# General path of a four-layer FNet and linear-attention kernel: input loads and output stores issued from ScalarE's queue instead of SyncE's

## The chip, the cores and the metric

The kernel runs on one NeuronCore of one Trainium2 chip. The metric is the device time of one execution in microseconds (us). Before the change three runs gave 745.84, 745.68 and 745.42 us, a median of 745.68 us.

## The reference

The input `x` is 2048 rows by 640 columns, float32. Four sublayers are applied in turn, each added to its own input: a Fourier layer, an attention layer, and both once more.

```python
x = x + _A_ref(_layernorm(x), dft_seq_re, dft_seq_im, dft_hid_re, dft_hid_im)
x = x + _B_ref(_layernorm(x), wqkv, wo)
# and the same two lines again

# _A_ref: y = Real(DFT_seq(DFT_hidden(x))), as dense products
a = einsum("bsd,ed->bse", x, dft_hid_re);  b = einsum("bsd,ed->bse", x, dft_hid_im)
y = einsum("ts,bse->bte", dft_seq_re, a) - einsum("ts,bse->bte", dft_seq_im, b)

# _B_ref: linear attention, 32 heads of 20, phi(t) = where(t > 0, t + 1, exp(t)) + 1e-6
kv = einsum("bhsd,bhse->bhde", phi(k), v);  z = einsum("bhsd->bhd", phi(k))
o = einsum("bhqd,bhde->bhqe", phi(q), kv) / (einsum("bhqd,bhd->bhq", phi(q), z) + 1e-6)
return o @ wo
```

The four Fourier matrices are inputs of the kernel, so the kernel may not assume what stands in them.

## The kernel before

The 2048 rows lie in 16 tiles of 128 rows (`X[0]` to `X[15]`), which stay on the chip through all four sublayers. The program has two ways to the result.

The fast path (`fast_path`, L1362 to L1453) uses the symmetries of a true Fourier matrix, which halve the products twice. While it computes, VectorE compares the whole Fourier matrices with their mirror images (class `Check`, L1324); `verdict` (L1331) reduces what it found to one integer, `ckflag`, during the last attention layer. The fast path loads `x` at L1372 and stores the result at L1424, both on SyncE's queue, which it has to itself: all 352 of the fast path's DMAs are issued there, in the order of the program. The order on the other engines is partly written out by hand, partly left to the planner, which simulates the schedule of a stretch of the program up to the next branch.

After the fast path, the flag is read by every engine into a register (L1502), and every engine branches on it (L1503):

```python
    bad = nc.values_load(flag, min_val=0, max_val=1)
    with tc.If(bad > 0):
        with ExitStack() as c2:
            general_path(k, c2, x, wqkv, wo, mask, (crt, cit, wrt, wit), out)
```

The general path (L1456 to L1484) does the whole computation again with plain dense products and overwrites the output. It is compiled into the program of every engine, between the branch and what follows it. An engine on which the flag is 0 jumps over it. Where it lands, a short stretch adds to the semaphores what the general path would have added: one instruction each on PE, DVE, ACT and POOL, and eight on SyncE, one for each of the eight semaphores that count DMA landings. Each of these eight first waits until all earlier DMAs counted by its semaphore have landed. Then come the closing instructions (marked L1626): on SyncE ten waits and three drains, on the others one or two of each, with two barriers over all engines.

Counted in the compiled program, the stretch that is jumped over holds 167 instructions on SyncE, 117 on DVE, 1015 on POOL, 1135 on ACT and 7310 on PE (each with its closing branch). SyncE's 167 are 95 DMA issues (16 loads of `x` at L1462, 20 of weights at L269, 12 at L526, 10 at L519, 20 small copies at L591, 17 stores at L1476), 71 instructions that only wait, and the branch. Three of the 71 stand ahead of the loads of `x` and one ahead of each store. ACT's 1135 contain 68 DMA issues already, for the Fourier matrices of the general path (L730, L754).

Of the kernel before, what the change touches and what calls it, by code (L numbers as in the profile page):

```python
# [17 lines left out]
HD = D // 2  # L18
# [1437 lines left out]
def general_path(k, ctx, x, wqkv, wo, mask, gen, out):  # L1456
    nc = k.nc
    xp = ctx.enter_context(k.tc.tile_pool(name="gxp", bufs=1))
    X = []
    for i in range(NT):  # L1460
        t = xp.tile([128, D], F32, name=f"gx{i}")
        nc.sync.dma_start(t, x[128 * i : 128 * i + 128, :])  # L1462
        X.append(t)
    order = list(range(NT))
    k.general, k.ve = True, Spared(k, ctx.enter_context(k.tc.tile_pool(name="near", bufs=3)))
    for layer in range(2):
        k.layer = 1
        layer_fourier_general(k, X, *gen)
        with ExitStack() as c2:
            for nm, b in (("tmp", 12), ("wp", 31), ("raw", 3), ("pqp", 16)):  # L1470
                setattr(k, nm, c2.enter_context(k.tc.tile_pool(name=k.nm(nm), bufs=b)))
            k.st = k.tmp

            def after(i, a, b):
                if layer == 1:
                    nc.sync.dma_start(out[128 * i : 128 * i + 128, HD * a : HD * b], X[i][:, HD * a : HD * b])  # L1476

            att = Attention(k, X, order, order, wqkv, wo, mask)
            for part in (1, 0):
                att.weights(part)  # L1480
            att.begin()
            att.begun()
            att.keys_values()
            att.outputs(after)  # L1484


@with_exitstack
def tile_kernel(
    ctx, tc, x, wqkv, wo, maskd, sign, ce, se, co, cex, wr, wi,
    ck0, ck1, ck2, ck3, ckr, cki, crt, cit, wrt, wit, out,  # L1490
):
    nc = tc.nc
    k = K(tc, ctx)
    mask = k.cst.tile([EC, EC], F32, name="mask")
    k.qd = ctx.enter_context(tc.tile_pool(name="qd", bufs=4))
    k.sm = ctx.enter_context(tc.tile_pool(name="sm", bufs=3))
    with ExitStack() as c2:
        c2.enter_context(tc.manual_schedule(engines={mybir.EngineType.SP}))
        flag = fast_path(
            k, c2, x, wqkv, wo, (mask, maskd), sign, (ce, se, co), cex, (wr, wi), (ck0, ck1, ck2, ck3), (ckr, cki), out  # L1500
# [5 lines that stand above are left out]
# [126 lines left out]
```

## Time and profile before

| what | value |
|---|---|
| median of three runs | 745.68 us (745.42 to 745.84) |
| the profiled execution's own time | 747.02 us |
| its span, first to last instruction | 745.0 us |
| outside the span | 2.0 us |
| busy share PE, DVE, ACT, POOL | 97%, 80%, 52%, 35% |
| granted TensorE clock, mean | 0.996 |
| instructions executed | 12,890 |
| DMA traffic of SyncE's queue | 104.20 MB |

An engine's name with a q (SPq, PEldq) means its sequencer, the part that waits, branches and issues DMAs. SP is SyncE. Rows of one line of code give the instruction, how often it ran, shortest, middle and longest duration in ns, and the start of the first and last in us. The rows of the profile with kind "instruction" are the DMA packets by which the engines fetch their own program.

### The profile page before, as it was taken

To read this page: it belongs to the slowest core of one execution; us is meant where nothing else is said; L and a number is where in the kernel's file an instruction comes from. 1 tells how busy PE (TensorE), PEld (TensorE's weight loads), DVE (VectorE), ACT (ScalarE), POOL (GpSimd) and SP (SyncE) were. 2 spreads that over 40 slices of the span, in tenths; PEclk is the share of its full clock that TensorE was granted. 3 is DMA by queue.
4 is the path that set the end of the run, shared out by engine and by line. 5 is a ranking of instruction groups with operands and counts; after the bars stand their busy time and mean duration, and the time that the engine had idled before them with its cause. 6 is when DMAs were issued, how large, how long until landed. Compare 5 with 4: busy or idle time off the path is not lost.

```text
span 745.0 us, 12890 instructions
## 1 busy us (share of the span) xinstructions
PE 723.1 (97%) x4762; PEld 691.4 (93%) x4762; DVE 599.6 (80%) x1147; ACT 384.4 (52%) x723; POOL 262.5 (35%) x293
## 2 busy tenths in 40 slices
PE   4999999999999999999999999999999999999997
PEld 1389999999999999899986999999999999999996
DVE  7998988868779786888987876967787887689973
ACT  7745654665445644455775347566532554453320
POOL 4237941331024311567772672136000010153310
PEclk9999999999999999999999999999999999999999
DMA  9332457562776826420001463654156653102653
GB/s 329 103 91 89 130 165 244 179 202 67 241 223 209 269 97 197 152 93 1 10 10 54 145 233 91 211 162 148 37 163 198 189 187 119 56 12 72 194 162 109
DMA packets 59006, 105.10 MB, mean 141 GB/s; under 512 B 5652, under 2 KB 23319, under 8 KB 58935
## 3 DMA queue, kind: packets, MB, share of 16 engines
q1 hardware_dynamic: 58935, 104.20, 43.8%
q8 instruction: 40, 0.66, 0.4%
q14 instruction: 31, 0.25, 0.1%
HBM read 78.99 MB, written 24.78 MB: 139 GB/s over the span
## 4 chain that ended last, share of the span: by engine, by line
PE 71%; DVE 15%; ACT 5%; DMA 3%; issue 2%; POOL 2%; SPq 1%; DVEq 0%; ACTq 0%; POOLq 0%
PE ps L250 48%; PE ps L355 16%; PE ps L1173 3%; PE ps L1099 2%; PE ps L201 1%; DVE w L189 1%; DVE t L189 1%; DMA raw<-in_wo 1%; DMA x<-in_x 1%; DVE t L622 1%; DVE ab L992 1%; DVE ps L615 1%; DVE x L644 1%; DMA raw<-in_wqkv 1%; PE ps L543 1%
## 5 line engine op out<-in xcount | busy, mean ns | idle before, releaser
L250 PE MATMUL ps<-w,t 128*128 128x320 f32 x2880 | 432.1, 310 | 0.6 <-DVE w L189 0.2
L250 PEld LDWEIGHTS ps<-w,t 128*128 128x128 f32 x2880 | 422.7, 188 | 1.9 <-DVE t L189 0.8
L355 PE MATMUL ps<-t,t 128*128 128x256 f32 (+1 forms) x640 | 139.8, 309 | 0.0
L1324 DVE CUSTOM_DVE_ANT_0 junk<-ck,ck 128x688 bf16<-128x688 f32 (+5 forms) x138 | 112.3, 813 | 7.4 <-DMA ck<-in_ck 6.2
L355 PEld LDWEIGHTS ps<-t,t 128*128 128x128 f32 x640 | 107.0, 188 | 0.0
L355 PE MATMUL ps<-w,t 128*128 128x384 f32 (+1 forms) x320 | 98.6, 310 | 0.6 <-DVE w L189 0.6
L388 ACT ACTIVATE t<-ps 128x640 f32<-128x640 f32 x64 | 45.0, 704 | 93.5 <-PE ps L250 90.0
L188 ACT CAST t<-t 128x640 fp32r<-128x640 f32 x62 | 45.1, 728 | 63.4 <-DVE t L218 28.5
L425 POOL TENSOR_TENSOR t<-t,s 128x640 f32<-128x640 f32 x17 | 30.5, 1793 | 117.1 <-DVE s L391 117.1
L599 POOL TENSOR_TENSOR t<-pq,t 128x640 f32<-128x640 f32 x25 | 40.1, 1612 | 74.6 <-ACT t L511 41.3
L355 PEld LDWEIGHTS ps<-w,t 128*128 128x128 f32 x320 | 60.1, 188 | 1.1 <-DVE w L189 0.9
L189 POOL TENSOR_TENSOR t<-t,t 128x640 fp32r<-128x640 f32 x14 | 23.1, 1646 | 92.7 <-ACT t L188 80.4
L189 DVE TENSOR_TENSOR t<-t,t 128x640 fp32r<-128x640 f32 x48 | 40.5, 845 | 15.9 <-ACT t L188 12.4
L391 DVE SCALAR_TENSOR_TENSOR pq<-t,pq 128x640 f32<-128x640 f32 x32 | 28.0, 876 | 24.7 <-ACT t L390 24.5
L390 ACT ACTIVATE t<-t 128x640 f32<-128x640 f32 x64 | 47.4, 741 | 0.0
L1173 PE MATMUL ps<-t,u 128*128 128x322 f32 x288 | 45.4, 314 | 0.4 <-DVE u L1156 0.4
L1173 PEld LDWEIGHTS ps<-t,u 128*128 128x128 f32 x288 | 43.2, 189 | 1.4 <-DVE u L1156 0.9
L188 ACT CAST t<-ps 128x640 fp32r<-128x640 f32 (+1 forms) x36 | 24.8, 690 | 36.0 <-PE ps L201 33.2
L391 DVE SCALAR_TENSOR_TENSOR s<-t,s 128x640 f32<-128x640 f32 x32 | 26.7, 835 | 16.2 <-ACT t L390 16.1
L1099 PE MATMUL ps<-cw,ab 128*128 128x512 f32 (+2 forms) x108 | 37.6, 500 | 1.7 <-ACT ab L962 1.0
L188 ACT CAST t<-s 128x640 fp32r<-128x640 f32 x32 | 23.3, 728 | 25.5 <-DVE t L189 18.6
L1099 PEld LDWEIGHTS ps<-cw,ab 128*128 128x128 f32 x108 | 19.9, 190 | 17.9 <-issue 12.6
(209 smaller groups left out, 1026.8 us busy)
## 6 DMA issues: line engine op xcount, KB each, us to landing
ck<-in_ck SPq DMA_DIRECT2D x48, 346.0 KB
ck<-in_ck SPq DMA_DIRECT2D x48, 344.0 KB
turn<-t SPq DMA_DIRECT2D x23, 320.0 KB
save<-w SPq DMA_DIRECT2D x20, 320.0 KB
w<-save SPq DMA_DIRECT2D x20, 320.0 KB
z<-turn SPq DMA_DIRECT2D x18, 320.0 KB
x<-in_x SPq DMA_DIRECT2D x16, 320.0 KB
out<-x SPq DMA_DIRECT2D x13, 320.0 KB
```

What stands on the lines that cost most here:

```text
L188: self.high = self.nc.scalar.copy(hi, src)
L189: return self.engine(pool).tensor_tensor(lo, src, hi.bitcast(F32), op=ALU.subtract)
L250: nc.tensor.matmul(pu[:m, 512 * h : 512 * h + HD], s, w[:, HD * h : HD * h + HD], start=first, stop=last)
L355: nc.tensor.matmul(self.place(G, c, part), x[:, 128 * c : 128 * c + 128], p[:, f : f + n], start=start and i == 0, stop=stop and i == 2, s ...
L388: nc.scalar.activation(h2(e), halves(pu), AF.Relu, scale=-1.0)
L390: nc.scalar.activation(e, e, AF.Exp, scale=-1.0)
L391: return k.ve.scalar_tensor_tensor(out, e, 1e-6, out, op0=ALU.add, op1=ALU.add)
L425: k.engine(n not in PKSUMS[k.layer]).tensor_tensor(pksum, pksum, pk, op=ALU.add)
L599: k.behind(k.nc.gpsimd.tensor_tensor(t1, self.PQ[self.order2[n]], self.zb, op=ALU.mult), lull)
L1099: self.k.nc.tensor.matmul(pu, s[:, cols : cols + 128], w[:, f : f + n], start=start and i == 0, stop=stop and i == len(todo) - 1)
L1173: self.k.nc.tensor.matmul(po[:, o : o + 322], s[:, f : f + 128], w[:, x, :], start=start, stop=stop)
L1324: i = nc.vector.tensor_tensor_reduce(k.junk[:, : a.shape[1]], b, a, 1.0, 0.0, op0, op1, o)
```

## The change

Two calls in `general_path` name another queue: `nc.scalar` (ScalarE, ACT) in place of `nc.sync` (SyncE, SP). Nothing else differs.

```diff
@@ -1459,7 +1459,7 @@
     X = []
     for i in range(NT):
         t = xp.tile([128, D], F32, name=f"gx{i}")
-        nc.sync.dma_start(t, x[128 * i : 128 * i + 128, :])
+        nc.scalar.dma_start(t, x[128 * i : 128 * i + 128, :])
         X.append(t)
@@ -1473,7 +1473,7 @@
             def after(i, a, b):
                 if layer == 1:
-                    nc.sync.dma_start(out[128 * i : 128 * i + 128, HD * a : HD * b], X[i][:, HD * a : HD * b])
+                    nc.scalar.dma_start(out[128 * i : 128 * i + 128, HD * a : HD * b], X[i][:, HD * a : HD * b])
```

`after` is called once for each of tiles 0 to 14 and twice, for the two halves, for tile 15.

## The prediction

> **What bounds the kernel now.** I looked first whether the changed lines run at all, then at the last microseconds.
>
> The page, its counts, its queues, and the loads and stores among the DMA issues:
>
> ```profile
> span 745.0 us, 12890 instructions
> PE 723.1 (97%) x4762; PEld 691.4 (93%) x4762; DVE 599.6 (80%) x1147; ACT 384.4 (52%) x723; POOL 262.5 (35%) x293
> q1 hardware_dynamic: 58935, 104.20, 43.8%
> q8 instruction: 40, 0.66, 0.4%
> q14 instruction: 31, 0.25, 0.1%
> x<-in_x SPq DMA_DIRECT2D x16, 320.0 KB
> out<-x SPq DMA_DIRECT2D x13, 320.0 KB
> out<-x SPq DMA_DIRECT2D x6, 160.0 KB
> ```
>
> And what the trace answers for the two changed lines:
>
> ```profile
> nothing on L1462; most used: ['L250', 'L355', 'L1173', 'L1099', 'L201', 'L1324', 'L189', 'L188', 'L543', 'L1294', 'L388', 'L391', 'L389', 'L390', 'L924', 'L213', 'L599', 'L218', 'L925', 'L209', 'L813', 'L425', 'L615', 'L500', 'L182']
> nothing on L1476; most used: ['L250', 'L355', 'L1173', 'L1099', 'L201', 'L1324', 'L189', 'L188', 'L543', 'L1294', 'L388', 'L391', 'L389', 'L390', 'L924', 'L213', 'L599', 'L218', 'L925', 'L209', 'L813', 'L425', 'L615', 'L500', 'L182']
> ```
>
> Sixteen loads of x and 13 + 6 stores are exactly the fast path's. The changed lines have no instruction in the trace: the flag was 0 and all engines jumped over the general path. PE is busy 97% of the span, and no DMA that is moved takes part in that. What the change can reach is only the jump and what follows it. So the next view is the chain of waits, its last pieces:
>
> ```profile
> 726.54 13.17 PE ps L250 x90
> 739.71 0.02 issue
> 739.74 0.49 DVE x L718
> ```
>
> The chain's work ends at 739.74 + 0.49 = 740.23 us, and the span at 745.0. Nearly 4.8 us at the end hold no arithmetic. They are the jump, told by the rows of the branch's line and, in the second fence, of the closing line:
>
> ```profile
> L1503 SPq EVENT_SEMAPHORE  x8: 17/17/17, 743.1 to 743.7; - x8
> L1503 POOLq COMPARE_BRANCH  x1: 45/45/45, 722.1 to 722.1; - x1
> L1503 POOLq EVENT_SEMAPHORE  x1: 17/17/17, 725.6 to 725.6; - x1
> L1503 ACTq COMPARE_BRANCH  x1: 50/50/50, 730.8 to 730.8; - x1
> L1503 ACTq EVENT_SEMAPHORE  x1: 17/17/17, 733.3 to 733.3; - x1
> L1503 PEldq COMPARE_BRANCH  x1: 4116/4116/4116, 737.8 to 737.8; - x1
> L1503 DVEq COMPARE_BRANCH  x1: 72/72/72, 740.4 to 740.4; - x1
> L1503 DVEq EVENT_SEMAPHORE  x1: 21/21/21, 740.6 to 740.6; - x1
> L1503 SPq COMPARE_BRANCH  x1: 45/45/45, 740.6 to 740.6; - x1
> L1503 PEldq EVENT_SEMAPHORE  x1: 51/51/51, 742.0 to 742.0; - x1
> ```
>
> ```profile
> L1626 SPq EVENT_SEMAPHORE  x10: 17/28/28, 743.7 to 745.0; - x10
> ...
> L1626 SPq DRAIN  x3: 7/7/13, 744.2 to 744.5; - x3
> ```
>
> SP branches at 740.6 and does its first instruction behind the jump at 743.1, 2.5 us later. Its eight additions run to 743.7, its closing instructions to 745.0, 1.3 us more. The other engines were through at 725.6, 733.3, 740.6 and 742.0. SP is the last by 1.7 us: its jump sets the end.
>
> Set the gap between branch and next instruction beside the length of what is jumped over: DVE 117 instructions, 0.2 us; SP 167, 2.5; POOL 1015, 3.5; ACT 1135, 2.5; PE 7310, 4.2. Only the shortest jump is quick. I read the others as waits for the engine's own program to be fetched; the queues of kind "instruction" bring it in packets of 0.25 MB / 31 = 8 KB and 0.66 MB / 40 = 16 KB. The waits of SP's queue name no other engine for this gap:
>
> ```profile
> SPq L1503 <- SPq L1503: 2.5, 1, 2.5
> ```
>
> One cause would compete: the first addition may wait for the last store rather than for code. The store's issue, and the DMA traffic of the end (columns behind the busy times: clock, DMA share, GB/s):
>
> ```profile
> 740.25 0.33 SPq L1424 DMA_DIRECT2D out<-x  x1
> ...
> 741.00:741.50 0.50, 0.00 (x0) 0.00 (x0) 0.00 (x0) 0.00 (x0) 0.00 (x0) 1.00 0.80 289
> 741.50:742.00 0.50, 0.00 (x0) 0.00 (x0) 0.00 (x0) 0.00 (x0) 0.00 (x0) 1.00 0.20 65
> 742.00:742.25 0.25, 0.00 (x0) 0.00 (x0) 0.00 (x0) 0.00 (x0) 0.00 (x0) 0.73 0.00 0
> 742.25:742.50 0.25, 0.00 (x0) 0.00 (x0) 0.00 (x0) 0.00 (x0) 0.00 (x0) 0.50 0.00 0
> 742.50:743.00 0.50, 0.00 (x0) 0.00 (x0) 0.00 (x0) 0.00 (x0) 0.00 (x0) 0.50 0.17 33
> ```
>
> By 742.0 the store's 160 KB have gone (289 and 65 GB/s over 0.5 us each make 177 KB). And of the eight semaphores the last store counts on the eighth alone, since the 352 DMAs take turns over them; the first addition had nothing young to wait for, yet it too stood until 743.1.
>
> **The change part by part.**
>
> *The moved DMAs.* 16 loads and 17 stores leave SP's stretch for ACT's. None is executed: 0 us, and nothing is queued behind them, on SP or on ACT. The cover is the flag. Were it 1, the 33 issues would cost ACT about 33 x 0.33 us = 11 us at the store's issue time above, and the whole general path would be added; no row hints at that.
>
> *SP's jump gets shorter.* With the loads go the three waits ahead of them, with the stores the 17 ahead of those: 167 - 16 - 3 - 17 - 17 = 114 instructions left, a few more if new waits are needed. The trace has no jump of 114. Its price lies between the rows of DVE (117 instructions, 0.2 us) and SP itself (167, 2.5 us). I take 0.2, because 114 is nearest to 117. The upper end, 2.5, is no change at all.
>
> Where the wait goes: SP would reach its additions at 740.6 + 0.2 = 740.8 or 740.9, and seven of them at SP's pace of (743.7 - 743.1) / 7 = 0.09 us take it to about 741.5. The eighth waits for the last store. That is late next, together with PE's jump, which ends at 742.0 and which SP's closing waits need. The store's data have gone by 742.0; its signal comes after that, by how much no row says. The bound above is SP's longest wait for a store of 320 KB near the end, from that store's issue to SP's next DMA:
>
> ```profile
> 721.83 0.39 SPq L209 DMA_DIRECT2D turn<-s  x1
> ...
> 725.25 0.33 SPq L213 DMA_DIRECT2D s<-turn  x1
> ```
>
> That is 3.4 us; from 740.25 it gives 743.65, when the eighth addition runs already now, so nothing would be gained. The bound below is 742.0, PE's jump and the end of the data. I take 742.3, near the lower end, because half the bytes move here and the traffic is visibly over. The eighth addition goes from 743.7 to 742.3, and the 1.3 us behind it stay: saving 1.4 us, with bounds of 1.7 and 0.
>
> [...]
>
> *ACT's jump gets longer*, 1135 to some 1190. It already pays the long price, 730.8 to 733.3; POOL's 3.5 us is the most among jumps of that order. It could grow by 9 us before it reaches 742.0: 0 us.
>
> *The fast path's schedule.* The stretch up to the branch is planned by itself and its instructions are the same: 0 us. The eight semaphores remain SP's to raise: ACT issues 68 DMAs in the general path already, and all eight additions are on SP.
>
> Sum against the profiled execution: 747.0 (span 745.0 and 2.0 around it) - 1.4 = 745.6 us, span 743.6. The median of the runs is 1.3 us under the profiled time; the same difference taken from it gives 745.7 - 1.4 = **744.3 us**, 0.19% less.
>
> **The rivals.**
>
> *Nothing changes* (chance 0.33): 745.7 us. The quick jump of DVE may be quick because its target happened to lie in the same packet of code, and a target in the following packet may be fetched again whatever the distance; or the 2.5 us aren't code at all. For it: one quick jump among five is thin. Against it: four slow ones, all longer, and a first addition that stands for nothing else. [...]
>
> *A second fetch* (0.05), which ends on the other side. The target is fetched after all, as now, and lies just before the end of its packet. Then SP stands again within its 8 + 13 instructions behind the jump. Now those run from 743.1 to 745.0 without a stop. A second fetch that starts when the first is in, at 743.1, and takes another 2.5 us is in at 745.6; if it is needed for the first closing wait (743.7 now), the end moves by 745.6 - 743.7 = 1.9 us, to 747.6. It decides from the point at which the packet ends early enough among the 21 instructions; for the very last ones it costs 0.6 us, 746.3. For it: the target moves by 53 instructions, so it may fall anywhere in a packet. Against it: it takes two things at once, a fetch in spite of the short jump and a packet's end within the 21 instructions.
>
> *The planner's order moves* (0.02): if the longer ACT stretch changed what is laid out before the branch, PE, at 97%, would feel it either way: 0.2% of 745 is 1.5 us, 744.2 to 747.2. The unchanged instructions speak against it.
>
> *The short jump* is the rest, 0.60; its own range is 743.9 (the 1.7 us bound and the spread of the three runs) to 744.9.
>
> **How the numbers follow.** A measurement of this kernel can tell about 0.2%, 1.5 us, from no change. The short jump's 1.4 us lies just under that line: I give it 0.35 to be over, since the store's signal may come earlier than 742.3 and the bound is 1.7. That makes 0.60 x 0.35 = 0.21, with 0.01 from the planner, 0.22 for faster. Slower by over 0.2% needs a second fetch that falls early, 0.03, and 0.01 from the planner. Within 0.2% is the rest, 0.74. The range reaches from 744.0 over the unchanged time to 745.9; it leaves out the fastest ends of the short jump and the second fetch.
>
> **What would show it.** In the profile after: still nothing on the two changed lines; SP's first addition at about 740.9 in place of 743.1; the eighth a step later than the other seven, at 742.0 to 742.5; SP's closing instructions 1.3 us long as now; PE's jump to 742.0, ACT's to 733.3. Wrong would be: a gap of 2.5 us on SP behind the branch as before (nothing changes), a gap among the closing instructions (second fetch), an eighth addition near 743.6 (the store is late), or any moved start before 737 us (the planner).

## The result, and the profile after

The changed kernel takes 744.70 us (median of 15 runs, 743.56 to 745.54), the kernel before 745.91 us beside it (15 runs, 745.28 to 747.49). The ratio is 0.998, with a 95% interval of 0.9972 to 0.9988: 0.9 to 2.1 us less, some 1.5.

The same rows of the branch's line as before, now of the changed kernel (instruction, count, shortest, middle and longest duration in ns, first and last start in us):

```profile
L1503 SPq EVENT_SEMAPHORE  x8: 17/17/17, 740.4 to 741.3; - x8
L1503 POOLq COMPARE_BRANCH  x1: 45/45/45, 721.8 to 721.8; - x1
L1503 POOLq EVENT_SEMAPHORE  x1: 17/17/17, 725.3 to 725.3; - x1
L1503 ACTq COMPARE_BRANCH  x1: 50/50/50, 730.3 to 730.3; - x1
L1503 ACTq EVENT_SEMAPHORE  x1: 17/17/17, 732.8 to 732.8; - x1
L1503 PEldq COMPARE_BRANCH  x1: 3696/3696/3696, 737.0 to 737.0; - x1
L1503 DVEq COMPARE_BRANCH  x1: 72/72/72, 739.6 to 739.6; - x1
L1503 DVEq EVENT_SEMAPHORE  x1: 21/21/21, 739.8 to 739.8; - x1
L1503 SPq COMPARE_BRANCH  x1: 45/45/45, 739.9 to 739.9; - x1
L1503 PEldq EVENT_SEMAPHORE  x1: 51/51/51, 740.8 to 740.8; - x1
```

SP's first instruction behind the jump comes 0.5 us after its branch, where it came 2.5 us after it. ACT (2.5 us), POOL (3.5) and DVE (0.2) jump as before. The same row, asked for two stretches of time, takes the eight additions apart:

```profile
L1503 SPq EVENT_SEMAPHORE  x7: 17/17/17, 740.4 to 740.9; - x7
```

```profile
L1503 SPq EVENT_SEMAPHORE  x1: 17/17/17, 741.3 to 741.3; - x1
```

Seven run at SP's pace, the eighth is 0.4 us late: it waits for the last store, whose landing stands in the trace at 741.26 us, just ahead of it. Before the change the store landed at 742.27, 0.8 us ahead of SP's first addition, so it was not what that addition waited for. The closing instructions and the span:

```profile
L1626 SPq EVENT_SEMAPHORE  x10: 17/28/28, 741.3 to 742.6; - x10
```

```profile
span 742.7 us, 12890 instructions
```

```profile
738.95 0.02 issue
738.97 0.49 DVE x L718
```

The last fence is the end of the chain of waits. From SP's branch to the end of the span it was 745.0 - 740.6 = 4.4 us and is now 742.7 - 739.9 = 2.8: the change is worth 1.6 us. The rest of the span's 2.3 us lies ahead of the branch: the arithmetic ends at 739.46 in place of 740.23. The order of PE's and DVE's instructions is the same in both programs, and over the profiles below, which have that order too, SP's branch comes anywhere from 738.5 to 740.9; so nothing shows that this part comes from the change. For this reason the experiments are read by the stretch from branch to end, and the ratios beside it.

The packets by which the engines fetch their program agree with this. The DMA queues of the kernel before, in the 1.5 us from SP's branch (queue, kind: packets, MB, share of 16 engines):

```profile
q1 hardware_dynamic: 151, 0.17, 33.7%
q14 instruction: 1, 0.01, 1.9%
```

One 8 KB packet of code comes in. It begins at 741.56 us, 0.93 behind the branch, is in at 742.00, and SP goes on 1.1 us later. In the changed kernel, from its branch to its first addition (0.5 us), the same view has one row, and none of the kind "instruction":

```profile
q1 hardware_dynamic: 11, 0.01, 6.9%
```

There the next 8 KB packet begins at 741.02, 0.6 us behind the first addition, when SP is already at work behind the jump.

### The profile page after: what moved, and what is told of

It is laid out like the page before. It is cut to its first block, busy times and chain, and to the rows that moved or that the text cites. A ratio compares the mean times of both kernels' runs of the same rounds, so it can differ in the third digit from the quotient of the medians.

```text
span 742.7 us, 12890 instructions
## 1 busy us (share of the span) xinstructions
PE 722.4 (97%) x4762; PEld 691.3 (93%) x4762; DVE 599.4 (81%) x1147; ACT 384.4 (52%) x723; POOL 262.9 (35%) x293
## 4 chain that ended last, share of the span: by engine, by line
PE 77%; DVE 11%; ACT 5%; DMA 2%; issue 1%; POOL 1%; SPq 1%; DVEq 0%; POOLq 0%; ACTq 0%
PE ps L250 49%; PE ps L355 16%; PE ps L1173 6%; PE ps L1099 4%; PE ps L201 2%; DVE w L189 1%; DVE t L189 1%; DMA raw<-in_wo 1%; DVE t L622 1%; DVE ps L615 1%; DVE ab L992 1%; DMA x<-in_x 1%; DVE x L644 1%; PE ps L543 1%; ACT ab L961 1%
```

## The experiments

Theory, to be tested: what counts is where SP's jump lands. SP goes on quickly (0.5 us, as after the change) when the target lies in the packet of code that it is in or in the next one, and otherwise stands for a fetch (2.5 us, as before it). Rivals: the queue of the moved DMAs is what counts; or the length of the jump alone. To count instructions, SP's branch is the 570th of its program in both kernels, the target the 738th before and the 685th after (the branch by the instructions of SP in the trace, the target by adding the length of the jump).

**Length restored.** The changed kernel, its general path padded on SP to 167 instructions:

```diff
+    ... [nc.sync.dma_start(dp.tile([1, 128], F32, name=f'pad{i}'), x[0:1, 0:128]) for i in range(53)]; ...
```

> The changed kernel with 53 tiny loads (512 bytes, from x to a spare place in memory, never used) added to the general path on SP, so that SP's jump is 167 instructions long again as before the change; like the rest of the general path they are not executed. Theory (the length and place of SP's jump are the whole effect): the first addition behind the jump comes 2.5 us after the branch again in place of 0.5, and the time goes back to that of the kernel before, ratio 1.000 within 0.1%. Rival (what counts is that the x loads and stores are on ACT's queue): the gap stays 0.5 us and the ratio 0.998.

Measured: ratio 0.9992 (0.9981 to 1.0002), 745.69 us against 746.20. Rows of the padded kernel:

```profile
L1503 SPq EVENT_SEMAPHORE  x8: 17/17/17, 741.0 to 741.6; - x8
...
L1503 SPq COMPARE_BRANCH  x1: 45/45/45, 738.5 to 738.5; - x1
```

The gap is 2.5 us again, and with the span's 742.9 us the stretch from branch to end 4.4, as before the change, with the x loads and stores still on ACT's queue. The rival of the queue falls by this; the ratio alone, with an interval from 0.9981, would not have told. (The early branch, 738.5, shows the spread ahead of it.)

**Other DMAs moved.** The kernel before, with its weight loads moved in place of the x loads and stores:

```diff
-        self.k.nc.sync.dma_start(raw, src)
+        (self.k.nc.scalar if self.k.general else self.k.nc.sync).dma_start(raw, src)
-            nc.sync.dma_start(t, self.wqkv[2][128 * c : 128 * c + 128, :])
+            (nc.scalar if k.general else nc.sync).dma_start(t, self.wqkv[2][128 * c : 128 * c + 128, :])
```

> The kernel before, x loads and stores of the general path left on SP; in their place its weight loads (L269 and L519) go to ACT's queue. SP's jump is 122 instructions. Theory: quick jump, 0.5 us, ratio 0.998; its target is eight instructions nearer to the end of its packet of code than in the changed kernel, so SP may stand for some tenths of a us among the closing instructions. Rival (the x loads and stores themselves): 2.5 us, ratio 1.000.

Measured: ratio 0.9983 (0.9970 to 0.9997), 744.65 us against 746.20.

```profile
L1503 SPq EVENT_SEMAPHORE  x8: 17/17/17, 739.5 to 740.6; - x8
...
L1503 SPq COMPARE_BRANCH  x1: 50/50/50, 739.0 to 739.0; - x1
```

The same gain from other DMAs: gap 0.5 us, branch to end 742.0 - 739.0 = 3.0 us. The stop among the closing instructions, which the expectation thought possible, is not there: they run for 1.3 us, as before the change and after it:

```profile
L1626 SPq EVENT_SEMAPHORE  x10: 17/28/28, 740.7 to 742.0; - x10
```

**Half of the change: the stores alone.** The kernel before, with this edit:

```diff
-                    nc.sync.dma_start(out[128 * i : 128 * i + 128, HD * a : HD * b], X[i][:, HD * a : HD * b])
+                    nc.scalar.dma_start(out[128 * i : 128 * i + 128, HD * a : HD * b], X[i][:, HD * a : HD * b])
```

> Only the stores are moved to ACT's queue, the loads of x stay on SP. SP's jump is 133 instructions. Length theory: between 114 (quick) and 167 (slow), open. Place theory: SP holds the packet of code that it is in and the next one; counted through the program the branch is its 570th instruction and the target the 704th. [...] The fetches of before fit packets that end near 576 and 704, so the target is the last of its packet or the first of the one after it: either a gap of 2.5 us and the time of before, or a gap of 0.5 us with a second stop of about 1 to 2 us behind it, and a time between the two kernels, ratio 0.998 to 1.001.

Measured: ratio 0.999 (0.9979 to 1.0000), 745.05 us against 746.20. The jump is quick:

```profile
L1503 SPq EVENT_SEMAPHORE  x8: 17/17/17, 739.4 to 740.3; - x8
...
L1503 SPq COMPARE_BRANCH  x1: 50/50/50, 738.9 to 738.9; - x1
```

But the closing instructions, in two stretches of time, show a second stop:

```profile
L1626 SPq EVENT_SEMAPHORE  x8: 27/28/28, 740.4 to 740.9; - x8
```

```profile
L1626 SPq DRAIN  x3: 7/7/133, 741.5 to 741.9; - x3
```

The eight additions are the 704th to the 711th instruction, the eight closing waits the 712th to the 719th. They run to 740.9, then SP stands for 0.6 us, between its 719th and its 720th instruction. From branch to end it is 742.4 - 738.9 = 3.5 us, between the two kernels; the ratio's interval reaches both the full gain and no gain.

**The other half: the loads alone.** The kernel before, with this edit:

```diff
-        nc.sync.dma_start(t, x[128 * i : 128 * i + 128, :])
+        nc.scalar.dma_start(t, x[128 * i : 128 * i + 128, :])
```

> Only the loads of x are moved to ACT's queue, the stores stay on SP. SP's jump is 148 instructions, its target the 719th of SP's program. Place theory with packets that end near 704: 2.5 us, ratio 1.000 within 0.1%. If moving half of the change gave half of the gain instead, the ratio would be 0.999.

Measured: ratio 1.0004 (0.9993 to 1.0016), 746.49 us against 746.20. The time is as expected, the way there isn't. The branch, and the additions in two stretches of time:

```profile
L1503 SPq COMPARE_BRANCH  x1: 45/45/45, 740.3 to 740.3; - x1
```

```profile
L1503 SPq EVENT_SEMAPHORE  x1: 17/17/17, 740.8 to 740.8; - x1
```

```profile
L1503 SPq EVENT_SEMAPHORE  x7: 17/17/17, 743.0 to 743.5; - x7
```

The first addition comes quickly, 0.5 us behind the branch, and the second 2.2 us after the first. The target was the 719th instruction, and again the stop lies between the 719th and the 720th. I read it as the edge of a packet: the engine had the 719th at hand and stood for the 720th. By both halves an edge lies behind 719, not behind 704 as I had put it; 576 and 704 were my estimate. In both halves the trace has the next 8 KB packet beginning 0.6 us behind the first addition; with the stores alone SP had 15 more instructions to run meanwhile, with the loads alone none. The gain is not shared out between loads and stores: by the stretch from branch to end, one half of the change alone gives about half of it, the other half nothing.

**The place alone.** The kernel before, the general path untouched, with 24 idle loads on SP's queue in the fast path where SP stands still:

```diff
+    def extra(self): self.fetched = getattr(self, 'fetched', 0) + 1; [self.k.nc.sync.dma_start(self.k.dram.tile([1, 128], F32, name=f'spare{i}'), self.hid[0][0][0:1, 0:128]) for i in range(24 if self.fetched == 11 else 0)]
     def hidden_fetch(self, par, c):
-        raw = self.k.raw.tile([128, 322], F32, tag="raw", name=self.k.nm("rawh"))
+        self.extra(); raw = self.k.raw.tile([128, 322], F32, tag="raw", name=self.k.nm("rawh"))
```

> The kernel before, without the change, but with 24 tiny loads (512 bytes, memory to memory, never used) on SP's queue in the fast path, at 322 us where SP stands still for 47 us; they are executed. SP's jump stays 167 instructions long; only its place moves, the branch from the 570th to the 594th instruction, the target from the 738th to the 762nd. Place theory (packets of 128 that end near 576, 704 and 832; the one the engine is in and the next are held): branch just behind 576, target ahead of 832, so a gap of 0.5 us in place of 2.5 and a ratio of 0.998 with no change to the general path at all. Length theory (167 is too far wherever it lies): 2.5 us, ratio 1.000.

Measured: ratio 0.9975 (0.9965 to 0.9985), 744.67 us against 746.72.

```profile
L1503 SPq EVENT_SEMAPHORE  x8: 17/17/17, 740.2 to 741.2; - x8
...
L1503 SPq COMPARE_BRANCH  x1: 45/45/45, 739.7 to 739.7; - x1
```

A jump of 167 instructions, and a gap of 0.5 us; branch to end 742.6 - 739.7 = 2.9. More work on the queue makes the kernel as fast as the change does. The ratio says a little more than the 1.5 us of the stretch; part of that is likely the granted clock, 0.9974 on average in the runs of the kernel before beside it and 0.9988 in its own, where runs of the kernel before at 0.993 and 0.994 took 748.9 us and those at 1.000 took 745.5 to 746.5. That the loads ran, ahead of the branch and in SP's idle time, is seen in the timeline of the same kernel (start, duration, what):

```profile
319.72 16.06 SPq L1102 DMA_DIRECT2D spare<-in_wr  x24
367.77 0.34 SPq L1105 DMA_DIRECT2D rawh<-in_wi  x1
```

**The place to within three instructions.** The same with 21 in place of 24:

```diff
-... for i in range(24 if self.fetched == 11 else 0)]
+... for i in range(21 if self.fetched == 11 else 0)]
```

> As the kernel before with 24 tiny loads in the fast path, but with 21. The runs on the stores alone and the loads alone showed SP's stop behind the 719th instruction of its program, so packets of an estimated 128 end behind the 591st and the 719th. With 21 the branch is the 591st, the last of its packet; the next packet ends at 719 and the target is the 759th. Place theory: 2.5 us again and ratio 1.000, although the program differs by three idle loads from the one that had a gap of 0.49 us and 0.9975. Rival (the added loads as such make the kernel faster, by what they do to the DMA queues or the memory): 0.5 us and 0.9975.

Measured: ratio 1.0003 (0.9993 to 1.0013), 746.40 us against 746.32.

```profile
L1503 SPq EVENT_SEMAPHORE  x8: 17/17/17, 743.1 to 743.7; - x8
...
L1503 SPq COMPARE_BRANCH  x1: 45/45/45, 740.7 to 740.7; - x1
```

Three idle loads fewer, and the 2.5 us and the time of before are back; length is the same in both, so the rival of length falls, and so does any good that the idle loads might do by themselves. The edge that this pair straddles lies behind the 591st, 592nd or 593rd instruction, and the two halves have one behind the 719th: the two are 126 to 128 of SP's instructions apart, which I read as one packet of 8 KB; the expectations had put 128. The trace of the kernel before gives an estimate of the same size: between 66.7 and 718.7 us queue q8 brought 35 packets of 16 KB, and PE ran 4417 products and 4415 weight loads. If q8 is PE's, that is 252 of these instructions to 16 KB, or 126 to 8 KB.

**Inside one packet.** The changed kernel with 8 idle loads, and then with 24:

```diff
+    def extra(self): ... for i in range(8 if self.fetched == 11 else 0)]
```

> The changed kernel with 8 such tiny loads in the fast path: branch at the 578th instruction, target at the 693rd, by the place theory in the same packet. The gap should fall from 0.5 us to about the 0.2 of DVE, if the other 0.3 are the step to the next packet; the time stays that of the changed kernel within 0.1% (ratio to before 0.998), since the eighth addition waits for the last store anyway. If the 0.5 us are SP's own pace, the gap stays 0.5.

Measured: ratio 0.9986 (0.9975 to 0.9997), 745.45 us against 746.72; against the expectation the gap stayed 0.5 us:

```profile
L1503 SPq EVENT_SEMAPHORE  x8: 17/17/17, 741.4 to 742.4; - x8
...
L1503 SPq COMPARE_BRANCH  x1: 50/50/50, 740.9 to 740.9; - x1
```

The place had been worked out from an edge behind 576; with the true one some 15 instructions later the branch (578th) and the target (693rd) still lay on two sides of it. The run decides nothing on the 0.5 us; with 24 idle loads both lie in one packet:

```diff
+    def extra(self): ... for i in range(24 if self.fetched == 11 else 0)]
```

> The changed kernel with 24 tiny loads in the fast path: branch at the 594th instruction, target at the 709th, now in the same packet (592 to 719). If the 0.5 us of the changed kernel are the step into the next packet, the gap falls to DVE's 0.2; the end stays where the last store's landing puts it, 2.8 us behind the branch, ratio to before 0.998. If 0.5 us are SP's own pace, the gap stays 0.5.

Measured: ratio 0.9992 (0.9983 to 1.0001), 745.92 us against 746.32.

```profile
L1503 SPq EVENT_SEMAPHORE  x8: 17/17/17, 740.7 to 742.1; - x8
...
L1503 SPq COMPARE_BRANCH  x1: 50/50/50, 740.6 to 740.6; - x1
```

The target (709th) is in the branch's packet. In steps of 0.05 us, the branch lies between 740.55 and 740.60 and the first addition between 740.70 and 740.75: a gap of 0.1 to 0.2 us, as short as DVE's. The 719th instruction is now the third closing wait. The closing waits in two stretches of time:

```profile
L1626 SPq EVENT_SEMAPHORE  x3: 28/28/28, 742.2 to 742.3; - x3
```

```profile
L1626 SPq EVENT_SEMAPHORE  x7: 17/28/28, 742.7 to 743.8; - x7
```

Between the third and the fourth SP stands for 0.4 us, the step over the edge. The trace has the next 8 KB packet in at 739.86, ahead of the branch, and none between the branch and this step, so I take the code to have been at hand. The expectation had left that out: it now lies behind the store's landing, where nothing hides it, and branch to end takes 743.9 - 740.6 = 3.3 us. The quicker jump makes the slower end.

**What is late next.** The last tile's result stored once, 320 KB, in place of twice 160 KB, in the changed kernel and in the kernel before:

```diff
-        nc.sync.dma_start(out[128 * i : 128 * i + 128, HD * a : HD * b], X[i][:, HD * a : HD * b])
+        (i, b) == (15, 1) or nc.sync.dma_start(out[128 * i : 128 * i + 128, 0 if i == 15 else HD * a : HD * b], X[i][:, 0 if i == 15 else HD * a : HD * b])
```

> The changed kernel with the last tile's result stored once, 320 KB behind the second half, in place of twice 160 KB. Theory (in the changed kernel the landing of the last store sets the end, by way of the eighth addition): the eighth addition and the end come later by about as long as 160 KB take, 0.4 to 0.7 us. Rival (PE's jump sets the end now): no later than in the changed kernel.

> The kernel before with the same single last store of 320 KB. Theory (SP's fetch sets the end before the change and covers the store): SP's first addition still 2.5 us behind its branch, the eighth right behind the seventh, the stretch from branch to end as long as before, 4.4 us, ratio 1.000. If the store set the end already, 0.4 to 0.7 us later.

Measured: ratios 0.9981 (0.9972 to 0.9990) and 0.9998 (0.9987 to 1.0010). The additions of the changed kernel with the large store, in two stretches of time, behind a branch at 739.7:

```profile
L1503 SPq EVENT_SEMAPHORE  x6: 17/17/17, 740.2 to 740.6; - x6
```

```profile
L1503 SPq EVENT_SEMAPHORE  x2: 17/17/17, 741.8 to 741.9; - x2
```

There is one DMA fewer, so the last store counts on the seventh semaphore. That addition comes 741.8 - 739.7 = 2.1 us behind the branch where the eighth came 1.4 behind it (741.3 - 739.9), and branch to end is 743.3 - 739.7 = 3.6 us in place of 2.8: the profile says that the store sets the end, at 0.7 to 0.8 us for 160 KB more (expected were 0.4 to 0.7). PE's jump does not set it, it was over at 740.5:

```profile
L1503 PEldq EVENT_SEMAPHORE  x1: 51/51/51, 740.5 to 740.5; - x1
```

The ratios, at intervals of 0.1% or 0.7 us to either side, can't tell 0.8 us.

In the kernel before, the branch is at 739.7 and the span ends at 744.7: 5.0 us, where I had expected 4.4.

```profile
L1503 SPq EVENT_SEMAPHORE  x8: 17/17/17, 742.8 to 743.3; - x8
```

The eight additions run without a stop, so it isn't the store that they wait for; but the gap is 3.1 us in place of 2.5. What came later is the packet of code. In the 1.5 us from SP's branch the view that showed a packet of q14 before the change has, with the larger store:

```profile
q1 hardware_dynamic: 143, 0.33, 56.2%
q8 instruction: 1, 0.02, 4.1%
```

No row of q14 yet, where one of 8 KB stood before the change. Its packet begins 1.56 us behind the branch in place of 0.93, right at the end of the store's data, and takes 0.31 us itself in place of 0.44: it starts later and is not slower. With the larger store in the changed kernel, too, the packet (there the following one, at 1.51 us in place of 1.14) begins right at the end of the store's data. Whether the code waits for the store's packets is not shown: both fit it, and no run isolates it.

All of it in one table, "branch to end" from SP's branch to the end of the span in the profile, in order of place:

| kernel | jump | branch, target | gap, us | branch to end, us | ratio to before |
|---|---|---|---|---|---|
| before | 167 | 570, 738 | 2.5 | 4.4 | 1 |
| padded | 167 | 570, 738 | 2.5 | 4.4 | 0.9992 (0.9981 to 1.0002) |
| before, 21 idle loads | 167 | 591, 759 | 2.5 | 4.4 | 1.0003 (0.9993 to 1.0013) |
| loads alone | 148 | 570, 719 | 0.5, then 2.2 | 4.6 | 1.0004 (0.9993 to 1.0016) |
| stores alone | 133 | 570, 704 | 0.5, then 0.6 | 3.5 | 0.9990 (0.9979 to 1.0000) |
| changed, 24 idle loads | 114 | 594, 709 | 0.2, then 0.4 | 3.3 | 0.9992 (0.9983 to 1.0001) |
| weights moved | 122 | 570, 693 | 0.5 | 3.0 | 0.9983 (0.9970 to 0.9997) |
| before, 24 idle loads | 167 | 594, 762 | 0.5 | 2.9 | 0.9975 (0.9965 to 0.9985) |
| changed, 8 idle loads | 114 | 578, 693 | 0.5 | 2.8 | 0.9986 (0.9975 to 0.9997) |
| changed | 114 | 570, 685 | 0.5 | 2.8 | 0.9980 (0.9972 to 0.9988) |

None of them beats the changed kernel by more than these intervals.

## Why the prediction was right

The mechanism was the forecast one, and the time lay 0.4 us from it: 744.7 against 744.3, inside the range. By the ratio the kernel is 0.2% faster, with an interval of 0.12% to 0.28% that does not reach no change. The saving lies on the 0.2% line that the forecast had called the least one can tell. Step by step:

- *The moved DMAs cost nothing.* Right. The trace of the changed kernel has no instruction on L1462 or L1476, and the padded kernel, with the DMAs moved, has the 4.4 us of before.
- *SP's jump falls from 2.5 to 0.2 us*, taken from DVE because 114 is nearest to 117. The direction was right, the size 0.5, and the reason only half of it. Length is not the rule: 167 was quick with 24 idle loads and slow with 21. A gap of 0.2 is what SP had inside one packet, with 24 idle loads in the changed kernel, and 0.5 is that of a step to the next; whether DVE's jump stays inside one packet isn't shown. A jump of 114 is shorter than the 126 to 128 instructions between two edges, so wherever it starts, its target lies in the same packet or the next. It was quick from the 570th, the 578th and the 594th instruction (0.5, 0.5 and 0.2 us), so by these runs it was not luck, though the one row of DVE could not tell that. By the length alone one could not have told 133 or 148.
- *Where the wait goes: the last store, at 742.3*, 1.7 us behind the branch. Right in kind (the eighth addition alone is late, and the larger store moves it), too long by 0.3: it came 1.4 us behind the branch. The landing in the trace of before, 742.27, is just where the forecast put it; over the ten traces with a last store of 160 KB it comes 1.4 to 1.7 us behind the branch, and the changed kernel's is at the early end, which is luck. So the saving from branch to end was 1.6 us, not 1.4. The 0.3 us too little on the jump cost nothing, since the store's landing covers it.
- *ACT's longer jump costs nothing.* Right: 730.3 to 732.8, 2.5 us as before, and 8 us of cover.
- *The sum.* 747.0 - 1.4 for the profiled execution; it was 744.55, since this execution was also quicker ahead of the branch by 0.7 us. The medians differ by 745.91 - 744.70 = 1.2 us, the ratio says 1.5. Of the 0.4 us by which the forecast missed the time, 0.2 is the kernel before itself, 745.9 us beside the change where the forecast started from 745.7.
- *The rival "nothing changes"* asked whether a target in the following packet would be fetched again whatever the distance. It isn't in these runs: the seven kernels whose target lies in the following packet have a gap of 0.5 us, and in the changed kernel no packet of code comes in between branch and first addition. Distance counts only by the edges: with a target beyond the following packet the gap was 2.5 us, and 3.1 with the larger store.
- *The rival "a second fetch"* exists, but not where the prediction put it. That had it follow a first fetch; the two halves of the change show it behind a quick landing. It costs 2.2 us when the edge comes right behind the target, 0.6 when it comes fifteen instructions later; in both the following packet begins 0.6 us behind the first addition, so it is under way while those fifteen run. The change was spared it: its 21 instructions run from the 685th to the 705th, fourteen short of the edge. That was luck, since the prediction did not know where the edges lie.

## What to carry to other kernels

Code that is not executed can still cost time when a branch jumps over it (on SP 2.5 us before the change, 0.5 after it): look at the gap between the branch and the next instruction on each engine, and at which engine comes through last. Here neither the kind of DMA that moved nor its queue was the cause, but the place of the landing, so a change of this size is easily taken for an effect of the queue that was edited; a control that restores the length, or moves the place alone, tells them apart. And when such a gap goes, the next late thing sets the end: SP's gap fell by 2.0 us, and 1.6 of them were gained, up to the landing of the last store.

## What the runs showed of the hardware

- Before the change one packet of code, 8 KB, came in during the 1.5 us behind SP's branch; SP went on 1.1 us after it was in. Read as edges of such packets, SP's stops put one behind its 719th instruction and one behind the 591st to 593rd, 126 to 128 apart.
- Counted by these edges, a jump cost 0.1 to 0.2 us inside a packet (one run), 0.5 into the next one (seven kernels), and 2.5 beyond it (three kernels).
- A jump that landed on the 719th instruction, the last ahead of an edge, was quick for one instruction (0.5 us) and then stood for 2.2 us.
- With the last packet of code in at 739.86, ahead of the branch at 740.6, the step over the edge behind the 719th took 0.4 us (one run).
- With a last store of 320 KB rather than 160 KB the same jump took 3.1 us in place of 2.5: the packet of code began 1.56 us behind the branch in place of 0.93.
- Between profiles of programs with the same order on PE, SP's branch came at 738.5 to 740.9 us. That spread is larger than the effect, which only the stretch behind the branch shows cleanly.
